# Three rotating places for queries and keys, and loads placed by the attention planner, in a fused attention, mixture and feed-forward kernel

## The chip, the cores and the metric

One core of a Trainium2 chip runs the whole program in one launch. The metric is the device time of one execution in microseconds (us); lower is better. The kernel before takes 396.39 us, the median of three runs (395.87 to 397.82).

## The reference

Three parts follow one another: windowed attention with a bias by distance, a soft mixture of experts whose dispatch is a softmax over all tokens, and a feed-forward layer with a squared ReLU. All data are float32.

```
# q, k, v: 4 batches, 8 heads, 576 positions, 64 wide
scores = q @ k.T / 8 - slope[h] * |i - j|     where 0 <= i - j < 128, else masked
attn   = softmax(scores) @ v                  -> x: 2304 tokens x 512
logits = x @ phi                              # 32 slots: 8 experts x 4
slots  = softmax(logits over tokens).T @ x
slots  = relu(slots[e] @ w1[e]) @ w2[e]       # 8 experts, 512 -> 1024 -> 512
x      = softmax(logits over slots) @ slots
out    = relu(x @ w_in) ** 2 @ w_out          # 512 -> 2048 -> 512
```

## The kernel before

Attention works in 16 **units** (a batch and a pair of heads) of 9 chunks of 64 queries. Two chunks make a **step**, 72 in all, so a unit has four and a half. For a step t, called S(t), T(t) and so on below:

- `emit_S` (L178, PE): the scores of two chunks, with up to 192 keys each; a chunk's Q is the weights (tile `zq`), K the moving side (`kt`). A float32 matmul shows as two passes in the trace, so a step has four.
- `emit_max` (L187, DVE) adds the bias and takes the row's extreme; `emit_exp` (L196, ACT) exponentiates and sums; `emit_sums` (L201, POOL) and `emit_recip` (L206, DVE) make the reciprocals, for two steps together except at either end; `emit_fold` (L220, POOL) and `emit_norm` (L228, POOL) fold and normalise p. Six buffers of p take turns.
- `emit_T` (L242, PE) transposes p, `emit_evac` (L262 on ACT, L266 and L268 on DVE) brings it to `ptb`.

When a unit's steps are through, `emit_PV` (L278, PE) multiplies by V into `xa` and `xb`, `emit_xT` and `emit_xTb` bring the result to `xT`, and `emit_X` (L321), `emit_Y`, `emit_logits` (L308), `emit_logr` (L314) and `emit_d0` to `emit_d4` keep the running mixture of each batch. After attention come 16 steps with the first expert matrices (L747, tile H), 16 with the second (L886, tile O) and the feed-forward (L939 and L983).

**The order** of attention is made by a planner. `op` records each operation with its engine, an assumed duration, what it comes after, a due time, the PSUM banks that it takes and a lag. `arrange` plays them on four engines' clocks, and takes each time the one that can start first, by due time among equals. `run` issues them in that order.

**The loads** all go through SP's queue, in the order in which they are written, but for three that ACT issues at the start. SP waits at a load until its place is free, and what stands behind it waits too. Per unit they are Z (the queries, 576 KB), K (288 KB) and V (320 KB). Z has two places, `zq[0]` and `zq[1]`, K two of its own, V two. Unit 2 alone uses a third for Z and K, the ring tile `first`. Weights go through a ring of 19 tiles of 1024 KB. During attention the ring is filled with 19 weight tiles, as 38 halves of 512 KB (`load_half_w`); five more go to space that attention leaves (`load_extra`), and one to `yw`.

Loads are not known to the planner. `run` adds them behind other operations: after the S that has a unit's last chunk, Z and K of the next unit for that place and two or three halves; after `emit_xTb` of u, V of u+2. The arrivals of the first units stand as times in `landed`.

## Time and profile before

| | us |
|---|---|
| median of three runs | 396.39 |
| lowest and highest | 395.87, 397.82 |
| the profiled execution, its own time | 395.99 |
| its span, first to last instruction | 394.0 |
| TensorE (PE) busy | 383.5, 97% of the span |
| VectorE (DVE), ScalarE (ACT), GpSimd (POOL) busy | 273.8, 245.7, 118.0 |
| the granted TensorE clock, mean of the span | 1.000 of full speed |

A profile tells of one execution. A row of the order of time has a start, a length, the engine, a line of the kernel and what that line writes and reads, and in brackets the idle time ahead of it with what ended it. Matmuls are pipelined and their ends are modelled, so that the lengths of neighbours overlap: the distance of starts tells how fast they go. A row of the waits has the total, the number of times and the longest. Engine names ending in q are queues that issue transfers.

### The profile page before, as it was taken

To read this page: it belongs to the slowest core of one execution; us is meant where nothing else is said; L and a number is where in the kernel's file an instruction comes from. 1 tells how busy PE (TensorE), PEld (TensorE's weight loads), DVE (VectorE), ACT (ScalarE), POOL (GpSimd) and SP (SyncE) were. 2 spreads that over 40 slices of the span, in tenths; PEclk is the share of its full clock that TensorE was granted. 3 is DMA by queue.
4 is the path that set the end of the run, shared out by engine and by line. 5 is a ranking of instruction groups with operands and counts; after the bars stand their busy time and mean duration, and the time that the engine had idled before them with its cause. 6 is when DMAs were issued, how large, how long until landed. Compare 5 with 4: busy or idle time off the path is not lost.

```text
span 394.0 us, 7876 instructions
## 1 busy us (share of the span) xinstructions
PE 383.5 (97%) x2602; PEld 299.9 (76%) x2602; DVE 273.8 (69%) x814; ACT 245.7 (62%) x730; POOL 118.0 (30%) x291
## 2 busy tenths in 40 slices
PE   8899999998998999999999999999999999999996
PEld 7788788787785435687787887888877888888884
DVE  5676776685774786387867788887867785566455
ACT  4989888887985212287776766777567544433440
POOL 4878667667663052122111212101010000000000
PEclk9999999999999999999999999999999999999999
DMA  7989999899899999999303200000000040003004
GB/s 233 373 291 357 330 322 408 284 326 409 269 358 353 418 426 426 417 416 406 119 0 108 108 0 2 0 0 2 0 0 3 0 161 2 0 31 130 0 1 161
DMA packets 23225, 75.36 MB, mean 191 GB/s; under 512 B 2832, under 2 KB 4624, under 8 KB 21520
## 3 DMA queue, kind: packets, MB, share of 16 engines
q1 hardware_dynamic: 22608, 74.30, 50.1%
q10 hardware_dynamic: 576, 0.56, 0.4%
q8 instruction: 21, 0.34, 0.3%
q14 instruction: 20, 0.16, 0.1%
HBM read 70.13 MB, written 4.72 MB: 190 GB/s over the span
## 4 chain that ended last, share of the span: by engine, by line
PE 88%; DMA 7%; DVE 2%; POOL 1%; ACT 1%; issue 1%; SPq 0%; DVEq 0%; POOLq 0%; ACTq 0%
PE acc L983 49%; PE s L178 10%; PE xa L278 6%; PE h L939 4%; DMA kt<-in_k_dram 4%; PE tp L242 4%; PE O L886 4%; DMA yw<-in_w_dram 3%; PE H L747 2%; PE X L321 2%; PE MX L835 1%; DVE psum L1001 1%; PE L L308 1%; PE xb L278 1%; PE R L374 1%
## 5 line engine op out<-in xcount | busy, mean ns | idle before, releaser
L983 PE MATMUL acc<-whl,arena_gh 128*128 128x512 f32 x864 | 216.5, 393 | 0.0
L983 PEld LDWEIGHTS acc<-whl,arena_gh 128*128 128x128 f32 x864 | 160.1, 188 | 35.3 <-issue 2.9
L968 DVE TENSOR_TENSOR arena_gh<-hT,arena_gh 128x384 fp32r<-128x384 f32 (+1 forms) x97 | 53.7, 553 | 30.1 <-ACT arena_gh L964 24.2
L196 ACT ACTIVATE p<-p,st 128x192 f32<-128x192 f32 (+1 forms) x144 | 61.6, 432 | 8.6 <-DVE st L187 6.2
L951 ACT ACTIVATE acc<-h 128x384 f32<-128x384 f32 x47 | 23.2, 493 | 64.9 <-PE h L939 64.9
L795 POOL TENSOR_SCALAR yw<-f 128x512 f32<-128x512 f32 x32 | 27.3, 857 | 100.4 <-DVE arena_cin L812 53.5
L228 POOL TENSOR_SCALAR p<-p,st 128x128 f32<-128x128 f32 (+1 forms) x142 | 49.9, 371 | 16.2 <-DVE st L206 10.7
L178 PE MATMUL s<-kt,zq 128*128 128x192 f32 (+2 forms) x270 | 50.7, 325 | 2.6 <-DMA kt<-in_k_dram 2.6
L187 DVE CUSTOM_DVE_ANT_0 p<-s,tbl 128x192 f32<-128x192 f32 (+1 forms) x144 | 42.1, 324 | 10.2 <-PE s L178 6.1
L178 PEld LDWEIGHTS s<-kt,zq 128*128 128x128 f32 x270 | 41.4, 197 | 4.0 <-DMA zq<-in_z_dram 2.9
L939 PE MATMUL h<-cst_sb,Mst 128*128 128x384 f32 x95 | 32.2, 339 | 0.1
L262 ACT ACTIVATE ptb<-tp 128x256 f32<-128x256 f32 (+1 forms) x72 | 25.0, 357 | 8.6 <-PE tp L242 8.4
L266 DVE TENSOR_SCALAR ptb<-tp 128x256 f32<-128x256 f32 (+1 forms) x64 | 24.4, 385 | 8.2 <-ACT ptb L262 8.0
L242 PE MATMUL tp<-cs,p 128*128 128x128 f32 x144 | 26.7, 282 | 2.2 <-POOL p L228 2.0
L220 POOL TENSOR_TENSOR p<-p 128x128 f32<-128x128 f32 (+1 forms) x64 | 27.1, 424 | 4.2 <-ACT p L196 1.3
L278 PE MATMUL xa<-ptb,vt 128*64 128x256 f32 (+1 forms) x256 | 27.8, 359 | 0.0
L196 ACT ACTIVATION_READ_ACCUMULATOR p<-p,st 128x1 f32 x144 | 27.7, 193 | 0.0
L960 DVE TENSOR_TENSOR hT<-acc 128x384 f32<-128x384 f32 x17 | 9.5, 557 | 23.2 <-ACT acc L951 23.2
L964 ACT ACTIVATE arena_gh<-hT 128x384 fp32r<-128x384 f32 x48 | 24.8, 517 | 0.7
L278 PEld LDWEIGHTS xa<-ptb,vt 128*64 128x64 f32 x256 | 17.0, 136 | 10.2 <-issue 2.9
L964 ACT ACTIVATE arena_gh<-acc 128x384 fp32r<-128x384 f32 x47 | 24.2, 516 | 0.6
L810 DVE SCALAR_TENSOR_TENSOR yw<-f,yw 128x512 int32<-128x512 int32 x32 | 22.4, 706 | 0.8
(205 smaller groups left out, 454.2 us busy)
## 6 DMA issues: line engine op xcount, KB each, us to landing
w_w<-in_w_dram SPq DMA_DIRECT2D x38, 512.0 KB, 7.4
w_w<-in_w_dram SPq DMA_DIRECT2D x12, 1024.0 KB, 9.3
f<-in_w_in_dram SPq DMA_DIRECT2D x16, 512.0 KB, 9.9
f<-in_w_out_dram SPq DMA_DIRECT2D x16, 512.0 KB, 10.0
zq<-in_z_dram SPq DMA_DIRECT2D x13, 576.0 KB, 5.2
vt<-in_v_dram SPq DMA_DIRECT2D x16, 320.0 KB, 6.6
kt<-in_k_dram SPq DMA_DIRECT2D x13, 288.0 KB, 5.6
out_dram<-psum SPq DMA_DIRECT2D x11, 256.0 KB, 2.0
```

The source lines that it names most:

```text
L178: pe.matmul(out=sb_t[t][:, 256 * i:256 * i + n], lhsT=zbuf(u)[:, c].rearrange("p a b -> p (a b)"), rhs=kt_t[u][:, 64 * c + 64 - n:64 * c + ...
L187: dve.tensor_tensor_reduce(out=p, in0=sb_t[t][:, 256 * i:256 * i + n], in1=tbl[:, 192 * pr + 192 - n:192 * pr + 192], scale=-0.125, scalar ...
L196: act.activation(out=p, in_=p, func=AF.Exp, bias=st[:, k + i:k + i + 1], scale=-1.0, accum_out=st[:, 4 + k + i:5 + k + i])
L220: pool.tensor_tensor(out=ap(True), in0=ap(True), in1=ap(False), op=ALU.subtract)
L228: eng.tensor_scalar(out=p, in0=p, scalar1=st[:, k + i:k + i + 1], scalar2=0.0, op0=ALU.mult, op1=ALU.add)
L242: pe.transpose(A[:, i, :], P[:, o:o + 128], ident)
L278: pe.matmul(out=out, lhsT=v_t[u][:, j, po:po + 64], rhs=pt[:, a:b, po:po + 64], start=(j == 0 or (j == 3 and a == 2)), stop=(j == 4 or (j ...
L795: pool.tensor_scalar(out=y.bitcast(F32), in0=t[:, a, :, 1].bitcast(F32), scalar1=2.0 ** -112, scalar2=0.0, op0=ALU.mult, op1=ALU.add)
L939: pe.matmul(out=hb[-1][:, 0:HB], lhsT=Mst[:, 128 * f:128 * f + 128], rhs=cst_sb[:, c0:c0 + HB], start=True, stop=True)
L964: act.activation(out=lo_t[i][1][hf][:, 0, cl], in_=rbuf[hf][:, cl], func=AF.Square)
L968: eng.tensor_tensor(out=gh[hf][:, 1, cl], in0=g[hf][:, cl], in1=gh[hf][:, 0, cl].bitcast(F32), op=ALU.subtract)
L983: pe.matmul(out=acc_t[s], lhsT=gh[:, x, c0:c0 + 128], rhs=w[:, f % 2, y, :], start=(units[i] in firsts and a == 0), stop=(units[i] in last ...
```

## The change

Z and K get three places each, taken in turn by u modulo 3 (`zslot`); the third is the tile `first`. The last of the 19 weight tiles takes that tile's place in the ring, so it can go only when unit 14's scores are done.

Loads of Z, K, V and phi, and the 38 halves, become operations of the planner on a fifth clock, SP, that starts at 8.2 us. Z and K come after the scores of all earlier units of their place, V after P times V of u-2, a half tile at an assumed time of 15 us and 2.4 us more for each. S then comes after its Z and K, `emit_PV` after its V. Assumed durations of the sums and of P times V, the transposes' lag, and the due times of S, the reciprocals, X and its copy are changed.

```diff
--- before.py
+++ after.py
@@ -128,7 +128,9 @@
     zpool = zt.enter_context(tc.tile_pool(name="zpool", bufs=1, side="right"))
     more, sx = ExitStack(), ExitStack()
     NQ = 2
+    NZ = 1
     zq = [zpool.tile([128, NCH, 2, 64], F32, name=f"zq{i}") for i in range(NQ)]
+    kq = [zpool.tile([128, S], F32, name=f"kq{i}") for i in range(NQ)]
     tbl = ppool.tile([128, 768], BF16, name="tbl")
     NP = 6
     pbuf = [ppool.tile([128, 384], F32, name=f"p{i}") for i in range(NP)]
@@ -142,17 +144,20 @@
 
     first = ring.tile([128, 3 * S], F32, tag="w", name="first")
 
+    zq.append(first[:, 0:2 * S].rearrange("p (c a b) -> p c a b", c=NCH, a=2))
+    kq.append(first[:, 2 * S:3 * S])
+
+    def zslot(u):
+        return u % (NQ + NZ)
+
     def zbuf(u):
-        return first[:, 0:2 * S].rearrange("p (c a b) -> p c a b", c=NCH, a=2) if u == 2 else zq[(u if u < 2 else u - 3) % NQ]
+        return zq[zslot(u)]
 
     def load_z(u, c0=0, c1=NCH, eng=sp):
         eng.dma_start(out=zbuf(u)[:, c0:c1].rearrange("p c a b -> p (c a b)"), in_=z[u, :, 128 * c0:128 * c1])
 
     def load_k(u, c0=0, c1=NCH, eng=sp):
-        if u == 2:
-            kt_t[u] = first[:, 2 * S:3 * S]
-        elif c0 == 0:
-            kt_t[u] = zpool.tile([128, S], F32, tag="kt", name="kt", bufs=NQ)
+        kt_t[u] = kq[zslot(u)]
         eng.dma_start(out=kt_t[u][:, 64 * c0:64 * c1], in_=k[u, :, 64 * c0:64 * c1])
 
     def load_v(u):
@@ -417,6 +422,9 @@
     pool.memset(lgT, -1.0e30)
     ops, users = {}, {}
 
+    def load_phi(a):
+        sp.dma_start(out=phi_sb, in_=phi)
+
     def op(f, arg, eng, ns, after=(), due=0, banks=(), lag=100, at=0):
         ops[f, arg] = {"at": at, "eng": eng, "ns": ns, "after": [x for x in after if x], "due": due, "banks": banks, "lag": lag}
 
@@ -431,18 +439,29 @@
             owner[u, j], last[slot] = last.get(slot), u
     fin = {u: (NCH * u + NCH - 1) // 2 for u in range(NU)}
     alone = (0, 1, NS - 2, NS - 1)
-    landed = {0: 0, 1: 900, 2: 2600, 3: 3500, 4: 5000, 6: 6000, 9: 10500, 13: 13500}
+    landed = {0: 0, 1: 900, 2: 2600, 3: 3500, 4: 5000, 6: 6000, 9: 10500}
+    steps_of = lambda u: range(NCH * u // 2, fin[u] + 1)
+    for u in range(1, NU):
+        if u > 2:
+            before = [x for y in range(u) if zslot(y) == zslot(u) for x in each(emit_S, *steps_of(y))]
+            op(load_z, u, "SP", 1450, before, STEP * fin[u - 1] - 20000, (), 2300)
+            op(load_k, u, "SP", 740, before, STEP * fin[u - 1] - 19990, (), 2300)
+        op(load_v, u, "SP", 810, each(emit_PV, u - 2)[:u > 1], STEP * fin[u] - 6000, (), 2300)
+    op(load_phi, 0, "SP", 200, (), 9000, (), 2300)
+    for j in range(2 * RING):
+        late = [u for u in range(NU) if zslot(u) == NQ + j // 2 - (RING - NZ)]
+        op(load_half_w, j, "SP", 1260, [x for u in late for x in each(emit_S, *steps_of(u))], 16000 + 2400 * j, at=15000 + 2400 * j)
     for t in range(NS):
         ch, t0 = info[2 * t:2 * t + 2], STEP * t
         two = [(t, 0), (t, 1)]
         steps = (t,) if t in alone else (t - 1, t) if t % 2 else (t, t + 1)
-        op(emit_S, t, "PE", sum(4 * n / 2.4 + 12 for u, c, n, e in ch), (), t0 - 1500, (("S", each(emit_max, *two)),), 200, max(x for y, x in landed.items() if y <= t))
+        op(emit_S, t, "PE", sum(4 * n / 2.4 + 12 for u, c, n, e in ch), [(f, u) for f in (load_z, load_k) for u, c, n, e in ch if u > 2], t0 - 3000, (("S", each(emit_max, *two)),), 200, max(x for y, x in landed.items() if y <= t))
         for i, (u, c, n, e) in enumerate(ch):
             op(emit_max, (t, i), "DVE", n / 0.96 + 72, each(emit_S, t) + each(emit_T, *range(t - NP, t - NP + 1)[:t >= NP]), t0 + 100 * i, (), 108)
             op(emit_exp, (t, i), "ACT", n / 1.4 + 303, each(emit_max, (t, i)), t0 + 400 + 100 * i, (), 170)
         if t == steps[0]:
-            op(emit_sums, (t, len(steps)), "POOL", 274, each(emit_exp, *[(x, i) for x in steps for i in range(2)]), STEP * steps[-1] + 1500, (), 0)
-            op(emit_recip, (t, len(steps)), "DVE", 90, each(emit_sums, (t, len(steps))), STEP * steps[-1] + 1600, (), 120)
+            op(emit_sums, (t, len(steps)), "POOL", 350, each(emit_exp, *[(x, i) for x in steps for i in range(2)]), STEP * steps[-1] + 1500, (), 0)
+            op(emit_recip, (t, len(steps)), "DVE", 90, each(emit_sums, (t, len(steps))), STEP * steps[-1] + 600, (), 120)
         whole = sum(x[2] == 192 for x in ch)
         if whole:
             op(emit_fold, t, "POOL", 164 + 138 * whole, each(emit_exp, *two), t0 + 1500)
@@ -452,7 +471,7 @@
         full = [(u, (c - 1) // 2) for u, c, n, e in ch if c]
         half = [(u, c // 2 if c % 2 == 0 else c // 2 - 1) for u, c, n, e in ch if c != 1]
         free = lambda l: each(emit_PV, *[owner[x] for x in l if owner[x] is not None])
-        op(emit_T, t, "PE", 222, each(emit_norm, *two), t0 + 3500, (("T", each(emit_evac, *two[:1 + bool(half)])),), 200)
+        op(emit_T, t, "PE", 222, each(emit_norm, *two), t0 + 3500, (("T", each(emit_evac, *two[:1 + bool(half)])),), 230)
         op(emit_evac, (t, 0), "ACT", 52 + 106 * len(full), each(emit_T, t) + free(full), t0 + 4000, (), 135)
         if half:
             op(emit_evac, (t, 1), "DVE", (0, 208, 342)[sum(x[1] > 1 for x in ch)] + 208 * sum(x[1] == 0 for x in ch), each(emit_T, t) + each(emit_evac, (t, 0)) + free(half), t0 + 4300, (), 120)
@@ -461,7 +480,7 @@
         t0, odd, late = STEP * fin[u], b % 2, u == NU - 1
         parts = [(t, i) for t in range(NCH * u // 2, fin[u] + 1) for i in range(2) if (emit_evac, (t, i)) in ops]
         old = (each(emit_X, u - 4) + each(emit_logr, (u - 4) // NPAIR)) if 4 <= u < NU - 4 + 2 else []
-        op(emit_PV, u, "PE", 1840, each(emit_evac, *parts), t0 + 5500, (("xa", each(emit_xT, u)), ("T" if late else "B", each(emit_xTb, u))), 190, 9500)
+        op(emit_PV, u, "PE", 1910, each(emit_evac, *parts) + each(load_v, u)[:u > 0], t0 + 5500, (("xa", each(emit_xT, u)), ("T" if late else "B", each(emit_xTb, u))), 190, 9500)
         op(emit_xT, u, "ACT", 477, each(emit_PV, u) + old, t0 + 7400, (), 165)
         op(emit_xTb, u, "DVE" if late else "ACT", 104, each(emit_PV, u) + old, t0 + 7450, (), 165)
         if late:
@@ -469,8 +488,8 @@
         x_all = each(emit_xT, u) + each(emit_xTb, u)
         if u < NU - 2:
             tag = "T" if kk == NPAIR - 1 else "B"
-            op(emit_X, u, "PE", 436, x_all, t0 + 9000, ((tag, each(emit_xn, u)),), 170)
-            op(emit_xn, u, "DVE", 608, each(emit_X, u) + each(emit_d3, b - 1)[:b], t0 + 9500)
+            op(emit_X, u, "PE", 436, x_all, t0 + 8000, ((tag, each(emit_xn, u)),), 170)
+            op(emit_xn, u, "DVE", 608, each(emit_X, u) + each(emit_d3, b - 1)[:b], t0 + 12500)
             if odd:
                 op(emit_Y, u, "PE", 109, each(emit_X, u), t0 + 9010, (("T", each(emit_xr, u)),), 170)
                 op(emit_xr, u, "ACT", 175, each(emit_Y, u) + each(emit_d3, b - 1)[:b], t0 + 9500)
@@ -496,7 +515,7 @@
             for x in o["after"]:
                 users.setdefault(x, []).append(k)
         ready, seen, order = {k: o["at"] for k, o in ops.items()}, {}, []
-        clock = dict.fromkeys(("PE", "DVE", "ACT", "POOL"), 0)
+        clock = {"PE": 0, "DVE": 0, "ACT": 0, "POOL": 0, "SP": 8200}
         held = {tag: [] for tag in NBUF}
         can = {e: [k for k in ops if ops[k]["eng"] == e and not wait[k]] for e in clock}
 
@@ -541,26 +560,15 @@
         if f in (emit_logits, emit_logr):
             for u in units_of(a):
                 f(u)
+        elif f is load_half_w:
+            f()
         else:
             f(*(a if isinstance(a, tuple) else (a,)))
         if f is emit_S:
             if a in (1, 3):
                 keep_warm("B", 1, idle)
-            for u, c, n, e in info[2 * a:2 * a + 2]:
-                if c == NCH - 1:
-                    nu = u + (3 if u < 2 else 2)
-                    if u != 2 and nu < NU:
-                        load_z(nu)
-                        load_k(nu)
-                    if u == 0:
-                        load_v(1)
-                        sp.dma_start(out=phi_sb, in_=phi)
-                    for _ in range(0 if u == 0 else 3 if u % 2 == 0 or u == 15 else 2):
-                        load_half_w()
         if f is emit_T and a == 0:
             keep_warm("B", 2, idle)
-        if f is emit_xTb and a + NQ < NU:
-            load_v(a + NQ)
 
     left = {f: sum(k[0] is f for k in ops) for f in (emit_S, emit_T, emit_norm)}
     for f, a in arrange():
```

What this moves shows in the programs' orders. **SP's queue, from unit 6's V (before) and from behind unit 8's K (after) on.** `vt` is V, `zq` Z, `kt` or `kq` K, `w_w` weights; a w's two rows are its two halves.

Before:

```order
L160 DMA vt_790<-in_v_dram 128x640
L149 DMA zq1_93<-in_z_dram 128x1152
L156 DMA kt_836<-in_k_dram 128x576
L88 DMA w_w19_838<-in_w1_dram 128x1024
L82 DMA w_w19_838<-in_w1_dram 128x1024
L88 DMA w_w111_841<-in_w1_dram 128x1024
L160 DMA vt_889<-in_v_dram 128x640
L149 DMA zq0_92<-in_z_dram 128x1152
L156 DMA kt_933<-in_k_dram 128x576
L82 DMA w_w111_841<-in_w1_dram 128x1024
L88 DMA w_w113_936<-in_w1_dram 128x1024
```

After:

```order
L82 DMA w_w15_688<-in_w1_dram 128x1024
L165 DMA vt_772<-in_v_dram 128x640
L88 DMA w_w17_787<-in_w1_dram 128x1024
L82 DMA w_w17_787<-in_w1_dram 128x1024
L88 DMA w_w19_837<-in_w1_dram 128x1024
L157 DMA zq0_92<-in_z_dram 128x1152
L161 DMA kq0_94<-in_k_dram 128x576
L165 DMA vt_893<-in_v_dram 128x640
L82 DMA w_w19_837<-in_w1_dram 128x1024
L88 DMA w_w111_929<-in_w1_dram 128x1024
L157 DMA zq1_93<-in_z_dram 128x1152
```

Before, V of unit 6 stands first, then Z and K of unit 8, three halves, V of unit 7, and Z and K of unit 9 in the place of unit 7. After, that V is the second row; Z and K of unit 8 stand ahead of these rows, and those of unit 9 in the place of unit 6, ahead of unit 7's V.

**PE, from T53 to T56.** The names p count the six buffers (the changed program's numbers are two higher), so T54 reads the first, T53 the last.

Before:

```order
L242 MATMUL tp<-cs,p_100 128x128 x2
L178 MATMUL s<-kt,zq_93 128x192
L178 MATMUL s<-kt,zq_92 128x64
L178 MATMUL s<-kt,zq_92 128x128
L178 MATMUL s<-kt,zq_92 128x192 x3
L278 MATMUL xa<-ptb,vt 64x256 x6
L278 MATMUL xa<-ptb,vt 64x128 x2
L278 MATMUL xb<-ptb,vt 64x64 x4
L242 MATMUL tp<-cs,p_95 128x128 x2
L242 MATMUL tp<-cs,p_96 128x128 x2
L242 MATMUL tp<-cs,p_97 128x128 x2
```

After:

```order
L247 MATMUL tp<-cs,p_102 128x128 x2
L183 MATMUL s<-kq_94,zq_92 128x192
L183 MATMUL s<-kq_95,zq_93 128x64
L247 MATMUL tp<-cs,p_97 128x128 x2
L183 MATMUL s<-kq_95,zq_93 128x128
L183 MATMUL s<-kq_95,zq_93 128x192
L247 MATMUL tp<-cs,p_98 128x128 x2
L183 MATMUL s<-kq_95,zq_93 128x192 x2
L283 MATMUL xa<-ptb,vt 64x256 x6
L283 MATMUL xa<-ptb,vt 64x128 x2
L283 MATMUL xb<-ptb,vt 64x64 x4
L247 MATMUL tp<-cs,p_99 128x128 x2
```

Before, S58, S59 and S60 stand together, then P times V of unit 11 (`xa`, `xb`), then T54, T55 and T56. After, T54 stands between S58 and S59, T55 between S59 and S60, and T56 alone behind P times V.

**PE at the end of attention, after P times V of unit 14.**

Before:

```order
L242 MATMUL tp<-cs,p_99 128x128 x2
L308 MATMUL L<-xT_102,phi_sb 32x128 x4
L308 MATMUL L<-xT_103,phi_sb 32x128 x4
L308 MATMUL L<-xT_104,phi_sb 32x128 x4
L242 MATMUL tp<-cs,p_100 128x128 x2
L314 MATMUL L<-xT_102,phi_sb 32x64
L314 MATMUL L<-xT_103,phi_sb 32x64
L314 MATMUL L<-xT_104,phi_sb 32x64
L278 MATMUL xa<-ptb,vt 64x256 x6
```

After:

```order
L247 MATMUL tp<-cs,p_100 128x128 x2
L247 MATMUL tp<-cs,p_101 128x128 x2
L247 MATMUL tp<-cs,p_102 128x128 x2
L313 MATMUL L<-xT_104,phi_sb 32x128 x4
L313 MATMUL L<-xT_105,phi_sb 32x128 x4
L313 MATMUL L<-xT_106,phi_sb 32x128 x4
L319 MATMUL L<-xT_104,phi_sb 32x64
L319 MATMUL L<-xT_105,phi_sb 32x64
L319 MATMUL L<-xT_106,phi_sb 32x64
```

T71 (the sixth p) stood between the two kinds of logits (`L`) of units 12 to 14; now T69, T70 and T71 come first and both kinds of logits after them. T68 now stands ahead of P times V of unit 14.

**POOL at the end of attention, from the fold of step 68 on.**

Before:

```order
L220 TENSOR_TENSOR p_97<-p_97 128x64
L201 TENSOR_SCALAR st<-st 128x4
L220 TENSOR_TENSOR p_98<-p_98 128x2x64
L201 TENSOR_SCALAR st<-st 128x2
L228 TENSOR_SCALAR p_97<-p_97,st 128x128 x2
L228 TENSOR_SCALAR p_98<-p_98,st 128x128 x2
L220 TENSOR_TENSOR p_99<-p_99 128x2x64
L228 TENSOR_SCALAR p_99<-p_99,st 128x128
L201 TENSOR_SCALAR st<-st 128x2
L220 TENSOR_TENSOR p_100<-p_100 128x2x64
L228 TENSOR_SCALAR p_100<-p_100,st 128x128
```

After:

```order
L225 TENSOR_TENSOR p_99<-p_99 128x64
L206 TENSOR_SCALAR st<-st 128x4
L225 TENSOR_TENSOR p_100<-p_100 128x2x64
L233 TENSOR_SCALAR p_99<-p_99,st 128x128 x2
L233 TENSOR_SCALAR p_100<-p_100,st 128x128 x2
L206 TENSOR_SCALAR st<-st 128x2
L225 TENSOR_TENSOR p_101<-p_101 128x2x64
L233 TENSOR_SCALAR p_101<-p_101,st 128x128
L206 TENSOR_SCALAR st<-st 128x2
L225 TENSOR_TENSOR p_102<-p_102 128x2x64
L233 TENSOR_SCALAR p_102<-p_102,st 128x128
```

The sums of step 70 (`st` of 128x2) stood ahead of the norms of steps 68 and 69; now they stand behind them.

## Rows read from the trace of the kernel before

**Rows 1.** The chain of work that ended last, its shares by engine (the page).
```profile
PE 88%; DMA 7%; DVE 2%; POOL 1%; ACT 1%; issue 1%; SPq 0%; DVEq 0%; POOLq 0%; ACTq 0%
```

**Rows 2.** Busy us of each engine by stage; then clock, DMA share, GB/s.
```profile
15.00:118.10 103.10, 100.53 (x968) 82.91 (x968) 72.97 (x389) 88.84 (x372) 73.94 (x219) 1.00 0.94 337
...
131.70:165.00 33.30, 33.13 (x419) 16.12 (x420) 21.77 (x62) 6.33 (x14) 8.88 (x10) 1.00 1.01 422
165.00:394.00 229.00, 225.24 (x1032) 181.84 (x1030) 162.86 (x290) 135.07 (x290) 23.13 (x27) 1.00 0.19 76
```

**Rows 3.** Waits of PE over the span: us in total, times, longest.
```profile
PE s L178 <- DMA kt<-in_k_dram: 2.6, 3, 1.6
PE tp L242 <- POOL p L228: 2.0, 2, 1.3
```

**Rows 4.** Order of time on PE (start, us, what) around units 9 and 13.
```profile
62.10 0.49 PE L178 MATMUL s<-kt,zq 128*128 128x192 f32 x2
63.34 1.01 PE L178 MATMUL s<-kt,zq 128*128 128x64 f32 x6 [0.75 <-DMA kt<-in_k_dram]
...
66.67 0.82 PE L178 MATMUL s<-kt,zq 128*128 128x192 f32 x4
67.32 0.38 PE L242 MATMUL tp<-cs,p 128*128 128x128 f32 x2
...
91.86 0.49 PE L178 MATMUL s<-kt,zq 128*128 128x192 f32 x2
93.99 1.66 PE L178 MATMUL s<-kt,zq 128*128 128x64 f32 x10 [1.65 <-DMA kt<-in_k_dram]
```

**Rows 5.** The chain in order of time, at the same two places.
```profile
56.77 6.44 DMA kt<-in_k_dram
...
86.67 7.18 DMA kt<-in_k_dram
```

**Rows 6.** Order of time on SP's queue: one V and two Z loads.
```profile
45.80 0.33 SPq L160 DMA_DIRECT2D vt<-in_v_dram  x1
...
50.25 0.33 SPq L149 DMA_DIRECT2D zq<-in_z_dram  x1
...
80.21 0.33 SPq L149 DMA_DIRECT2D zq<-in_z_dram  x1
```

**Rows 7.** Order of time on PE and POOL around steps 48 and 49.
```profile
78.82 0.82 PE L178 MATMUL s<-kt,zq 128*128 128x192 f32 x4
...
85.01 0.60 PE L242 MATMUL tp<-cs,p 128*128 128x128 f32 x4
...
83.47 1.37 POOL L228 TENSOR_SCALAR p<-p,st 128x128 f32<-128x128 f32 x4
```

**Rows 8.** Order of time on PE and POOL at the end of attention.
```profile
120.47 0.86 PE L308 MATMUL L<-xT,phi_sb 128*32 128x128 f32 x24
121.44 0.44 PE L242 MATMUL tp<-cs,p 128*128 128x128 f32 x2
...
116.31 0.46 POOL L220 TENSOR_TENSOR p<-p 128x128 f32<-128x128 f32 x1
117.34 0.19 POOL L201 TENSOR_SCALAR st<-st 128x2 f32<-128x2 f32 x1 [0.58 <-ACT p L196]
117.63 1.43 POOL L228 TENSOR_SCALAR p<-p,st 128x128 f32<-128x128 f32 x4
```

**Rows 9.** Order of time on SP's queue and PE, from attention to experts.
```profile
112.80 0.33 SPq L160 DMA_DIRECT2D vt<-in_v_dram  x1
...
116.32 10.17 SPq L97 DMA_DIRECT2D w_w<-in_w_dram  x5
...
138.94 1.06 PE L747 MATMUL H<-yw,siT 128*32 128x512 f32 x8
```

**Rows 10.** Busy us by stretch, as in rows 2.
```profile
25.00:111.00 86.00, 83.60 (x809) 68.86 (x809) 62.02 (x327) 74.24 (x309) 60.81 (x180) 1.00 0.94 339
116.30:139.00 22.70, 21.01 (x215) 11.76 (x219) 14.60 (x66) 9.47 (x33) 5.09 (x14) 1.00 0.98 375
```

## The prediction

> **What bounds the kernel now.** I read the chain of waits first: it runs through TensorE for 88% of the span and through transfers for 7% [rows 1]. Then the stages. Attention (15 to 118.1 us) has TensorE busy 100.53 of 103.10 us, with no other arithmetic engine above 89; the expert layers 33.13 of 33.30; the last feed-forward 225.24 of 229.00 [rows 2]. So TensorE sets the time in every stage, and a change of order gains only what TensorE idles today, or loses idle time that it makes.
>
> The waits of TensorE name that idle time: scores waited for a K transfer 2.6 us in three waits, transposes for POOL's normalised p 2.0 us in two [rows 3]. The order of time shows where: scores stop at 62.10 us after two passes of unit 8's last chunk and go on with unit 9 at 63.34; the same from 91.86 to 93.99, unit 12 to unit 13 [rows 4]. The chain goes through K's transfers there, 6.44 us from 56.77 and 7.18 us from 86.67 [rows 5]. They were issued only then because with two places in turn Z and K of unit u wait until unit u-2 has been read.
>
> **The change, part by part.** *K's waits.* A step's four score passes take 0.65 us from start to start (66.67 to 67.32), 0.16 each [rows 4]. From 62.10 to 63.34 are 1.24 us for two passes, so 0.91 idle; from 91.86 to 93.99 are 2.13, so 1.80. The gaps that the rows print (0.75 and 1.65) are smaller because a matmul's end is modelled; they give the low end, 2.40. With three places unit 9's Z waits for unit 6 and unit 13's for unit 10. Z loads that wait for just these units were issued at 50.25 and 80.21 [rows 6], 12 us before the scores at 62.1 and 91.9, where the longer K needed 7.18 [rows 5]. In the new queue one V and four half tiles stand between unit 8's K and unit 9's Z; that V went at 45.80 [rows 6], so all of them can go before 50.25. The third wait (0.2 us) belongs to the first load and stays. Both others go: **-2.7**, between -2.4 and -2.7.
>
> *The order of TensorE.* Scores and transposes are the same instructions; they now alternate where two or three stood together. A transpose of step t needs POOL's norm of t. In the sum of instruction times the tightest new place is T54: from S54 to T54 lie 2.63 of scores, 0.88 of four transposes, 1.9 of P times V and 0.5 of X, 5.9 us. Before, T48 came 6.19 us after S48, and its two norms (the first half of four in 1.37 us from 83.47) were done 5.4 us after S48 [rows 7]. So the tightest transpose still has some 0.5 us, and the long leads are cut without making the short ones shorter. In the first steps T5 moves ahead of S9, to right behind the place where T4 waits for POOL: nothing at best, at worst a second wait like the one of 1.3 us there [rows 3]. For all new waits of transposes I take **+0.2**, between 0 and 1.3.
>
> *The tail.* POOL's norms of steps 68 and 69 no longer stand behind the sums of step 70, which wait 0.58 us for an exponential: they could start at 116.77, when the fold before them ends (116.31 and 0.46), instead of 117.63; 0.86 earlier, of which the same sums, now behind the norms, take back 0.2 [rows 8]. T71 at 121.44 hangs on that chain: -0.7. But the logits of units 12 to 14, 24 passes that the row at 120.47 gives 0.86 us, filled the wait for T71 and now stand behind it, ahead of the last P times V [rows 8]: +0.8 with the modelled end off. I take **+0.1**; it is -0.7 if the logits hide after all, and +0.9 if T71 comes no earlier.
>
> *The first expert layers.* The step that reads yw begins at 138.94 [rows 9], 7.2 us into a stage in which TensorE idles 0.17 us in all [rows 2]; that bounds the wait for yw. It goes if yw lands earlier by more than attention ends earlier: **-0.1**, or 0. After the last score SP now has one extra tile, both halves of the nineteenth ring tile (its place is freed by unit 14), four extra tiles and yw: seven tiles of 1024 KB, 7.34 MB. From 113.6 us (116.32, when the first extra tile went, less 2.7 [rows 9]) to 136.2, when yw is wanted, at the 375 GB/s of that stretch [rows 10] 8.5 MB can come; 1.1 MB (2.9 us) to spare, if nothing else is left in the queue. Ahead of it, V of unit 15 and one half tile, 0.85 MB, wait for P times V of unit 13; that V went at 112.80 [rows 9], so at 110.1 now, and is through by 113.6.
>
> *Loads of V, phi, weights.* V keeps its two places and its wait for P times V of u-2; phi, 64 KB, now goes behind V of unit 1, and only the logits behind unit 3 need it; half tiles are wanted after 131 us. Each costs an issue on SP, which does no arithmetic: 0. No instruction of DVE, ACT or POOL is added; they had 72.97, 88.84 and 73.94 of 103.10 us to do [rows 2], and do the same in 2.5 us less.
>
> Sum: -2.7 + 0.2 + 0.1 - 0.1 = -2.5, against the profiled execution's 395.99 us (its span is 394.0): 393.5. The median of the runs is 0.4 above that execution, which would give 393.9; I say **393.6**. All low ends together (-3.5) give 392.5, all high ones (-0.2) 395.8.
>
> **The rivals.** *Transfers become the bound (20%).* From 25 to 111 us the new queue has to bring ten Z and K (864 KB each), thirteen V and 34 halves (512 KB each: of 38, two go before 25 us, where five did, and two after unit 14): 30.9 MB, 360 GB/s. The old one moved 339 in that stretch, at 0.94 of the engines' time [rows 10]. For it: 339/0.94 is 361, so no more than what is asked. Against: the expert stage moved 422 [rows 2], and a queue that is asked ahead of time is deeper. At 339 it is 1.75 MB behind at 111 us; that is 4.7 us at 375, of which 2.9 are spare, and the expert layers wait 1.8: 395.3; without the spare, 396 and more. The three places still hide Z and K, so this rival gives the gain back late and not in attention.
>
> *A ceiling of the queue (3%).* If 361 GB/s is what such a mixture can reach, in the last stretch too, and the queue idles as before, 1.75 MB take 4.8 us and the 7.34 MB 20.3 of the 22.6 us there; the expert layers wait 2.5: 396.0. Against it stand the 422 GB/s over 33 us [rows 2]. The Trainium skill (DMA: Bandwidth & Descriptors, section Where 436 GB/s comes from) has such a rule, some 358 GB/s for one core's loads from HBM, which speaks against a plan that asks for 360; by the 422 the trace does not agree with it.
>
> *K's or V's wait returns at other units (10%).* The change would then not do what it says: SP issues in order, and a Z ready to go can stand behind a V that waits for P times V. Against: unit 6's V, ahead of unit 9's Z, was free to go 4.4 us before it [rows 6]. About 396, no change.
>
> *Transposes wait for POOL (12%): slower.* The place is the run of single transposes from T46 to T56, and T12 and T20, with leads of 6.0 to 6.3 us. If norms end later than that after the scores, each waits, and everything behind it. For it: the first norm of a pair needs the exponentials of the step behind it too, and ACT is busy 86% of the stage [rows 2]. Against: such waits were 2.0 us in all, at the start and in the tail [rows 3]. Six of them at 1.3 us, the longest there is, make 7.8: 393.5 + 7.8 = 401.3; four of them, 398.7. It decides from 5.8 us between a score and its norm on; T48 shows 5.4.
>
> **How the numbers follow.** Forecast 52% (392.5 to 395, of that nine tenths below 394.4), transfers 20%, returning waits 10%, transposes 12%, the ceiling 3%, something I did not see 3%. A measurement of this kernel tells 0.5%, 2 us, from no change. Faster by more than that: 0.47 of the forecast and 0.03 of the transfers' rival, 0.50. Slower: the transposes and 0.02 of the unseen, 0.14. The same: the rest, 0.36. The range leaves out the worst transposes and what is unseen: 392.0 to 397.0; it takes in both signs, and the likeliest case's own is 392.5 to 395.
>
> **What would show it.** Right: no wait of scores for K but the first; unit 9's first score follows unit 8's last within 0.2 us; the step that reads yw starts near 136.3 with no wait; the last stage is as long as before (229 us). Transfers: the expert layers wait for yw or an extra tile. Transposes: PE waits for POOL's p in dozens, not two. The forecast is wrong if attention's end (the first expert step) does not come 2 to 3.5 us earlier than 131.7, or if it does and the span does not follow.

## Result, and the profile after

The kernel after the change takes **392.11 us** (median; 391.52 to 393.32), the kernel before on the same chip 396.96 us (395.87 to 398.57): a ratio of 0.9877, interval 0.985 to 0.9905. Two later comparisons, on other chips, gave 393.06 against 396.22 (0.9893, 0.9853 to 0.9933) and 393.08 against 396.5 (0.9913, 0.9891 to 0.9935). So the change is faster by 3.2 to 4.9 us; 393.6 was predicted. The profiled execution's span is 389.7 us, where before's was 394.0.

TensorE's share of the chain of waits is now 92%, the transfers' 1%, where [rows 1] had 88 and 7. The page's line:

```profile
PE 92%; ACT 2%; DVE 2%; POOL 2%; DMA 1%; issue 1%; DVEq 0%; POOLq 0%; ACTq 0%
```

The stages, columns as in [rows 2] (busy us and instructions of each engine, then granted clock, DMA share, GB/s): attention, expert layers, last feed-forward, and the stretch of [rows 10].

```profile
15.00:112.00 97.00, 96.98 (x939) 81.05 (x939) 70.41 (x379) 85.48 (x361) 72.12 (x213) 1.00 0.95 356
127.80:160.70 32.90, 32.89 (x419) 16.24 (x420) 21.77 (x61) 6.33 (x14) 8.80 (x10) 1.00 1.02 421
160.70:389.70 229.00, 225.27 (x1032) 181.86 (x1031) 162.87 (x290) 135.14 (x290) 23.11 (x27) 1.00 0.19 74
25.00:111.00 86.00, 86.00 (x841) 71.66 (x840) 62.55 (x334) 75.77 (x319) 63.79 (x188) 1.00 0.97 366
```

In the last row TensorE is busy all of the 86.00 us, where it was 83.60 [rows 10], and the queue moves 366 GB/s for 339. The last feed-forward takes the same 229.00 us.

The waits of TensorE over the span (us in total, times, longest). Two of K are left, both in the first 7 us; those at units 9 and 13 [rows 4] are gone:

```profile
PE tp L247 <- POOL p L233: 2.0, 3, 1.0
PE warm L112 <- DVE acc L396: 1.1, 1, 1.1
PE s L183 <- DMA kq<-in_k_dram: 0.7, 2, 0.5
PE X L644 <- ACT dT L639: 0.5, 1, 0.5
```

In order of time, where units 8 and 9 meet and where steps now alternate with transposes (units 12 and 13):

```profile
60.91 0.49 PE L183 MATMUL s<-first 128*128 128x192 f32 x2
61.24 0.33 PE L183 MATMUL s<-kq,zq 128*128 128x64 f32 x2
...
90.42 0.66 PE L183 MATMUL s<-kq,zq 128*128 128x192 f32 x4
90.92 0.39 PE L247 MATMUL tp<-cs,p 128*128 128x128 f32 x2
91.14 0.71 PE L183 MATMUL s<-kq,zq 128*128 128x128 f32 x4
```

Unit 9's scores follow two passes of unit 8 by 0.33 us, 0.16 a pass, where [rows 4] have 1.24 us and a wait. The end of attention on TensorE, which answers to [rows 8]:

```profile
113.05 0.68 PE L247 MATMUL tp<-cs,p 128*128 128x128 f32 x2 [0.42 <-POOL p L233]
...
116.85 0.44 PE L247 MATMUL tp<-cs,p 128*128 128x128 f32 x2 [0.64 <-POOL p L233]
117.22 0.86 PE L313 MATMUL L<-xT,phi_sb 128*32 128x128 f32 x24
```

The last transpose comes first now, and the 24 passes of logits behind it, as the instruction order said.

One table carries what follows. All times are starts of TensorE's instructions in the order of time, in us: where step 4's first score starts; from there to the first expert step; from that to the step that reads yw; from the second expert layer's first step to the last matmul.

| execution | step 4 | to first expert step | to yw's step | rest |
|---|---|---|---|---|
| before | 9.86 | 121.86 | 7.22 | 242.02 |
| before, once more (f4) | 9.69 | 123.05 | 7.93 | 242.37 |
| after | 9.21 | 118.60 | 6.86 | 242.01 |
| after, once more | 9.57 | 118.55 | 7.78 | 241.99 |
| after, third (f3) | 9.51 | 118.55 | 8.16 | 242.04 |
| e1: three places alone | 9.60 | 119.18 | 6.86 | 242.03 |
| e3: all but the due times | 9.61 | 119.18 | 7.71 | 241.98 |
| e4: due times alone | 9.59 | 120.35 | 6.86 | 242.03 |
| f1: three places and due times | 10.37 | 118.55 | 7.44 | 241.99 |
| e2: the change with two places | 9.11 | 121.80 | 6.86 | 242.01 |
| f2: the change, halves earlier | 9.70 | 118.57 | 6.87 | 241.99 |
| f2 once more (g2) | 9.21 | 118.55 | 6.86 | 242.02 |
| g1: the change, halves later | 9.61 | 118.55 | 11.59 | 242.05 |

The second column repeats within 0.05 us among executions that give TensorE the same order and don't wait for a transfer. The first and the third vary from execution to execution; why, and what of it is the change's doing, is what the experiments had to say.

### The profile page after: what moved, and what is told of

It reads as the page before. It is cut to its first block, busy times and chain, and to the rows that moved or that the text cites. A ratio compares the mean times of both kernels' runs of the same rounds, so it can differ in the third digit from the quotient of the medians.

```text
span 389.7 us, 7880 instructions
## 1 busy us (share of the span) xinstructions
PE 381.3 (98%) x2602; PEld 299.3 (77%) x2602; DVE 273.7 (70%) x814; ACT 244.7 (63%) x730; POOL 117.9 (30%) x291
## 4 chain that ended last, share of the span: by engine, by line
PE 92%; ACT 2%; DVE 2%; POOL 2%; DMA 1%; issue 1%; DVEq 0%; POOLq 0%; ACTq 0%
PE acc L991 50%; PE s L183 10%; PE xa L283 6%; PE h L947 4%; PE tp L247 4%; PE H L755 4%; PE O L894 4%; PE X L326 2%; ACT p L201 1%; PE L L313 1%; PE MX L843 1%; DVE psum L1009 1%; PE xb L283 1%; POOL p L233 1%; PE R L379 1%; DMA kq<-in_k_dram 1%
## 5 line engine op out<-in xcount | busy, mean ns | idle before, releaser
L183 PE MATMUL s<-kq,zq 128*128 128x192 f32 (+2 forms) x198 | 38.1, 320 | 0.7 <-DMA kq<-in_k_dram 0.7
L183 PEld LDWEIGHTS s<-kq,zq 128*128 128x128 f32 x198 | 30.3, 194 | 1.7 <-DMA kq<-in_k_dram 1.2
L247 PE MATMUL tp<-cs,p 128*128 128x128 f32 x144 | 28.1, 281 | 2.2 <-POOL p L233 2.0
L247 PEld LDWEIGHTS tp<-cs,p 128*128 128x128 f32 x144 | 18.2, 143 | 7.0 <-POOL p L233 4.8
```

The lines of the kernel that those rows point to most:

```text
L183: pe.matmul(out=sb_t[t][:, 256 * i:256 * i + n], lhsT=zbuf(u)[:, c].rearrange("p a b -> p (a b)"), rhs=kt_t[u][:, 64 * c + 64 - n:64 * c + ...
L247: pe.transpose(A[:, i, :], P[:, o:o + 128], ident)
```

## Experiments

**First, the change in parts.** On one chip, before at 396.22 us.

*e1: three places, due times as before.* The queue is still written by hand; Z and K of unit u+3 are asked for where those of u+2 were. TensorE's instructions come in the order of before.

```diff
+    kq = [zpool.tile([128, S], F32, name=f"kq{i}") for i in range(NQ)]
...
+    zq.append(first[:, 0:2 * S].rearrange("p (c a b) -> p c a b", c=NCH, a=2))
+    kq.append(first[:, 2 * S:3 * S])
...
-        return first[:, 0:2 * S].rearrange("p (c a b) -> p c a b", c=NCH, a=2) if u == 2 else zq[(u if u < 2 else u - 3) % NQ]
+        return zq[u % 3]
...
-                    nu = u + (3 if u < 2 else 2)
-                    if u != 2 and nu < NU:
+                    nu = u + 3
+                    if nu < NU:
```

> The old order of every engine and the old hand-written order of the queue, with three places for Z and K in turn. Theory A (the third place alone takes K's two waits away): no wait of scores for K at units 9 and 13, the first expert step 2.7 us earlier than 131.7, ratio 0.993, about 2.7 us less. Rival C (it takes the planner's queue, because halves stand ahead of Z): at least one of the two waits stays, ratio 0.998 to 1.0. Rival B (the new order of work makes most of the 4.3 us by which the spans differ) says no more than 1.5 us here.

Measured: 393.21 us (392.42 to 394.75), ratio 0.9894 (0.9851 to 0.9937). From step 4 to the first expert step 119.18 us, 2.68 less than before. Its one wait for K:

```profile
PE s L179 <- DMA kq<-in_k_dram: 0.2, 1, 0.2
```

The third place alone takes both waits away, and that is most of the gain. (The profile is of e1's slowest run, 394.75 us. What is slower there lies behind the last matmul, outside the table: the last two stores land after 4.2 us, in before's profile after 1.9.)

*e3: the change with the due times and durations of before.* The arithmetic engines get the order of before, the planner orders the loads.

```diff
-            op(emit_sums, (t, len(steps)), "POOL", 350, each(emit_exp, *[(x, i) for x in steps for i in range(2)]), STEP * steps[-1] + 1500, (), 0)
+            op(emit_sums, (t, len(steps)), "POOL", 274, each(emit_exp, *[(x, i) for x in steps for i in range(2)]), STEP * steps[-1] + 1500, (), 0)
...
-            op(emit_X, u, "PE", 436, x_all, t0 + 8000, ((tag, each(emit_xn, u)),), 170)
+            op(emit_X, u, "PE", 436, x_all, t0 + 9000, ((tag, each(emit_xn, u)),), 170)
```

The due times of the scores, the reciprocals and xn, the lag of the transposes and the duration of P times V go back in the same way.

> The changed kernel with the old due times and assumed durations: the order of PE, DVE, ACT and POOL is the old one, three places, and the queue ordered by the planner. Theory A: as the third place alone, ratio 0.993 within 0.002, since Z and K come in time either way. Rival C: 0.993 here but not with the hand-written queue. If the planner's queue also brings yw and the extra tiles sooner, up to 0.3 us more than with the hand-written queue.

Measured: 393.55 us (392.84 to 394.41), ratio 0.9908 (0.9875 to 0.9941). Attention takes 119.18 us, as in e1: who orders the queue changes nothing there. But TensorE waits for yw:

```profile
PE H L755 <- DMA yw<-in_w_dram: 0.6, 1, 0.6
```

*e4: before with the change's due times and durations,* the reverse of e3's edit; two places, queue by hand.

> The kernel before with the new due times and durations alone: the order of PE, DVE, ACT and POOL is that of the changed kernel, the queue and the two places are the old ones. Theory A: K's waits stay (2.4 us or more in two), the tail is 0.2 to 0.7 us shorter, T4 and T5 at the start change little: ratio 0.996 to 0.999. Rival B: the start and the tail give 1.5 us or more, ratio 0.996 or less, and with the third place's share the parts add to the whole.

Measured: 394.78 us (393.13 to 397.15), ratio 0.9955 (0.9925 to 0.9986). Attention 120.35 us, 1.51 less than before. K's waits stay, but shrink to 0.75 us at unit 9 and 0.56 at unit 13, where 2.4 or more in two was expected:

```profile
PE s L178 <- DMA kt<-in_k_dram: 1.5, 3, 0.7
```

Why they shrink wasn't tried.

*The change once more.*

> The changed kernel once more, on the same chip as its parts. Ratio 0.988 within 0.003. Its profile and those of the three others tell whether the first 9 us are the change's: TensorE's passes of 192 columns go from 0.32 to 0.16 us apart near 5 us in the changed kernel's profile and near 7.5 us in that of before, with the same instructions ahead. Theory A: this moment varies from one execution to the next, whatever the kernel, and the 0.6 us of it are not the change's. Rival: it goes with the order of work (early in this kernel and in the one with new due times alone, late in the two with the old order).

Measured: 393.06 us. Attention 118.55 us, 0.63 less than e1's, so the new order itself gains; and here, too, TensorE waits for yw, 0.7 us, which it did not in the first execution. By the medians, 393.06 and 393.21, the change was no faster than e1 on this chip. The trace has TensorE's full clock from 7.8 us on, not from 4.9 as in the first execution, with the same order of work: so the expectation's rival, that this moment goes with the order, fell. Two questions were left: does the order gain, and why does yw vary?

**Second: order and yw.** On one chip, before at 396.5 us.

*f1: e1 and e4 together,* that is the change's order and places with the hand-written queue.

> The kernel before with three places and with the new due times, but with its hand-written order of loads: TensorE, VectorE, ScalarE and GpSimd get the instructions of the change in the order of the change; the transfers are queued as in e1. Theory 1 (the queue that the planner writes costs the change 0 to 0.9 us at yw, and the new order of TensorE gains about 0.6 us before the expert layers): first expert step at 127.8 to 128.3 us, the step that reads yw 6.86 us behind it with no wait, and a time 0.3 to 0.9 us below the change's and 0.5 to 0.9 us below e1's, so some 392.3 where the kernel before is at 396.2. Theory 2 (the new order gains nothing, and the 0.66 us between e1 and the change is chance): first expert step at 128.6 to 128.9 like e1, time as e1's. Theory 3 (only the planner's queue lets the new order gain): a wait for K or V comes back, first expert step after 128.6 us.

Measured: 391.89 us (391.53 to 393.18), ratio 0.989 (0.9868 to 0.9912). Attention 118.55 us, exactly the change's, and 0.63 under e1's, which differs from it in the due times alone: the gain of the order is no chance. The first expert step came at 128.92, outside what was expected, because step 4 started as late as 10.37 (below). And yw was not free of waiting: 7.44, with a wait of 0.4 us. So theory 1 held for the order, and not for its "no wait": the hand-written queue, too, is at the edge. Yet by the medians of six runs each, whose ranges overlap, f1 is 1.2 us faster than the change on the same chip (393.08, in f3 below), more than the 0.3 to 0.9 that theory 1 had: the planner's queue did not gain, it cost.

*f2: one condition more in the planner.* The change makes half tile j wait, in the plan, for the units whose place is numbered NQ + j // 2 - 18. Only the nineteenth tile (j // 2 = 18) takes a place that Z and K had, the third. By the formula the seventeenth and eighteenth wait for the first two places as well; the first is used by unit 15, so two halves wait in the plan for the last scores. Half tiles are issued in the order of the ring, whichever j the plan calls, and so it is the nineteenth tile's halves that end up behind the first extra tile.

```diff
-        late = [u for u in range(NU) if zslot(u) == NQ + j // 2 - (RING - NZ)]
+        late = [u for u in range(NU) if j // 2 >= RING - NZ and zslot(u) == NQ + j // 2 - (RING - NZ)]
```

> The change with one condition more in the planner: half weight tiles whose place was never Z's or K's do not wait in the plan for scores. All four arithmetic engines get the change's order; SP issues all 38 halves before the first extra tile, where the change issues two (1 MB) behind it. Theory 1 (yw is late because 1 MB that could have gone in the hole from 96 to 103 us stands in the 8 us ahead of the last extra tiles): the step that reads yw comes 6.86 us after the first expert step, no wait of TensorE for yw or an extra tile, and 0 to 0.9 us less than the change on the same chip. Theory 2 (yw is late by the speed of the transfers in that execution, whatever stands ahead): 6.9 to 7.8 us here too, the change's time. Theory 3 (half tiles issued earlier stand in front of Z, K or V): a wait for K of over 0.3 us, and a first expert step later than the change's by as much.

Beside it the change again:

> The change itself once more, beside f1 and f2 on one chip. Both theories: 392 to 393.1 where the kernel before is at 396.2, ratio 0.988 to 0.991; first expert step 127.7 to 128.2 us; the step that reads yw 6.9 to 7.8 us later. The rise of TensorE's granted clock lay at 4.9 and at 7.8 us in two executions of it; if it is chance, it lies anywhere between here.

Measured: f2 391.88 us (six runs from 391.48 to 391.96), ratio 0.9886 (0.9867 to 0.9905); the change on that chip 393.08 (391.95 to 393.49). Attention is the same, 118.57 and 118.55; the whole of it is yw. SP's queue of the change in f3, in order of time, with the last half tiles (L88, L82) behind the first extra tile (L97), and the step of TensorE that reads yw:

```profile
112.72 0.33 SPq L97 DMA_DIRECT2D w_w<-in_w_dram  x1
113.10 0.43 SPq L88 DMA_DIRECT2D w_w<-in_w_dram  x1
113.57 0.43 SPq L82 DMA_DIRECT2D w_w<-in_w_dram  x1
...
117.69 0.33 SPq L97 DMA_DIRECT2D w_w<-in_w_dram  x1
...
136.22 1.06 PE L755 MATMUL H<-yw,siT 128*32 128x512 f32 x8 [1.09 <-DMA yw<-in_w_dram]
```

The same in f2:

```profile
110.19 0.42 SPq L82 DMA_DIRECT2D w_w<-in_w_dram  x1
112.93 0.33 SPq L97 DMA_DIRECT2D w_w<-in_w_dram  x1
117.92 0.33 SPq L97 DMA_DIRECT2D w_w<-in_w_dram  x1
...
135.13 1.07 PE L755 MATMUL H<-yw,siT 128*32 128x512 f32 x8
```

What the transfers do from 112 to 136 us, in 40 slices of 0.6 us (busy share in tenths, then GB/s). f3, the change:

```profile
DMA  8897798699999999997999999999999999989999
GB/s 137 273 314 239 253 355 328 280 355 300 328 376 410 389 403 416 403 341 287 423 410 382 423 437 410 437 423 437 437 423 423 437 423 437 389 355 416 430 403 423
```

And f2:

```profile
DMA  9939299940094999959999999999999998999999
GB/s 379 396 137 218 55 423 423 437 191 0 0 150 96 382 410 437 410 137 396 437 437 423 423 437 437 437 423 437 423 423 410 410 437 369 335 389 382 437 423 423
```

In f2 the queue runs empty near 117.5 us, before the last extra tiles and yw are asked for (from 120.6 on in f3, yw at 123.1 in f2); in f3 it never does. yw takes 13.3 us from issue to landing in f3, 10.0 in f2. The two halves of f2 went out at 96.47 and 97.49, ahead of a V that waits for P times V; SP stands at that V until 103.4, and in f3 from 96.2 to 103.2. What the transfers moved meanwhile (columns as in [rows 2]), f3 and then f2:

```profile
98.00:103.00 5.00, 5.00 (x69) 4.22 (x58) 3.53 (x24) 4.61 (x23) 2.85 (x9) 1.00 0.72 257
98.00:103.00 5.00, 5.00 (x70) 4.23 (x62) 3.74 (x24) 4.61 (x22) 2.87 (x9) 1.00 1.03 409
```

So 1 MB moved into a time in which the transfers had room is what separates a wait of 1.1 us from none. In the same 5 us the hand-written queues of e1 and f1 move 405 and 403 GB/s, the planner's, in the change's three executions, e3 and g1, 250 to 279.

*f4: before once more, for its profile.*

> The kernel before once more, for its profile alone. Theory 1 (the moment at which TensorE is granted its full clock in the first 9 us is chance, and no doing of the change): it can lie anywhere from 4.9 to 7.9 us here as well; whatever it is, K's two waits are 2.4 to 2.7 us and the first expert step comes at 131.2 to 131.8 us, the earlier the earlier the clock. Theory 2 (the change's first steps set it): it lies at 7.9 again and the first expert step at 131.7.

Measured, in its one run: 398.08 us. Step 4 starts at 9.69. K's waits are larger than in the first profile, and a fourth stands at unit 5 (0.3 us):

```profile
PE s L178 <- DMA kt<-in_k_dram: 3.5, 4, 1.6
PE tp L242 <- POOL p L228: 2.3, 3, 1.3
...
PE H L747 <- DMA yw<-in_w_dram: 0.9, 1, 0.9
```

Attention took 123.05 us, 1.2 more than in the profile that the prediction used, and the first expert step came at 132.74, where 131.2 to 131.8 was expected; yw was late here as well. Before's waits for transfers vary between its two profiles; that this is why its runs lie between 394.7 and 400.3 us, while f2's lie within half a microsecond, is likely and not shown.

**Third: the cost doubled, a repeat, and the third place taken away.** On one chip, before at 396.35 us.

*g1: more halves behind.*

```diff
-        late = [u for u in range(NU) if zslot(u) == NQ + j // 2 - (RING - NZ)]
+        late = [u for u in range(NU) if zslot(u) == (0 if j >= 32 else -1)]
```

> The suspected cost doubled: in the change, four half tiles (2 MB) instead of two (1 MB) are issued behind the first extra tile, and two of them behind the second; the order on the arithmetic engines is the change's. Theory 1 (what the queue has still to bring when the last extra tiles are asked for decides when yw comes): 1 MB more at 0.42 MB a us is 2.5 us; the step that reads yw comes 9.3 to 10.7 us after the first expert step, where the change had 6.9 to 8.2, and the time is 1.5 to 2.5 us over the change's: 394.5 to 395.5. Theory 2 (yw's time is chance): 6.9 to 8.2 us and the change's time, 392 to 393.5. From step 4's first score to the first expert step 118.55 us under both.

Measured: 398.0 us (396.55 to 399.27), ratio 1.0043 (1.0019 to 1.0067): slower than before. yw's step comes at 11.59. Theory 1 is right in kind and too low in size: six halves instead of three now stand behind V of unit 15, 1.57 MB more, not 1; at the 0.42 MB a us of that stretch 3.7 us, and 11.59 is 3.4 behind f3's 8.16. The profiled execution's span, 395.3 us, is 4.0 over f3's; another 0.5 of it lies between yw's step and the second expert layer, which come 9.50 us apart instead of 9.04. TensorE's waits:

```profile
PE H L755 <- DMA w_w<-in_w_dram: 2.7, 2, 1.9
...
PE H L755 <- DMA yw<-in_w_dram: 0.6, 1, 0.6
```

and the four microseconds around them (columns as in [rows 2]):

```profile
137.00:141.00 4.00, 3.19 (x16) 0.59 (x20) 1.61 (x3) 0.69 (x1) 1.74 (x2) 0.57 1.01 417
```

TensorE, which had waited 1.85 us before 137.26, ran these 4 us at a granted clock of 0.57, mostly the lower of its two levels (1.2 GHz), and at 1.00 again from 141 us on. The median is 0.8 us over the profiled run (397.18); the slowest runs have a mean clock of 0.991, the profiled one 0.996.

*f2 once more.*

> f2 once more, on another day of the chip. Theory 1: no wait for yw in this profile either, 6.87 us from the first expert step to the one that reads yw, and 391.5 to 392 where the kernel before is at 396.5. Theory 2: a wait of 0.4 to 1.1 us for yw in this profile, and 392.5 to 393.5. From step 4's first score to the first expert step 118.55 us under both.

Measured: 391.84 us (391.56 to 391.89), ratio 0.9871 (0.9838 to 0.9904); no wait for yw, 6.86. f2 beats the change and the kernel before.

*e2: the change with two places.*

```diff
     def zslot(u):
-        return u % (NQ + NZ)
+        return u if u <= 2 else (u - 3) % NQ
```

> The change with its third place taken away again (Z and K of unit 2 in the ring tile, all others in two places in turn); queue by the planner, new due times, orders on the arithmetic engines within some 20 rows of the change's. Theory 1 (K's waits hang on the number of places alone): TensorE waits for K at units 9 and 13 as in e4, 1.3 to 2 us in all; from step 4's first score to the first expert step 119.9 to 120.6 us, where the change has 118.6, and a time 1.2 to 2 us over the change's. Theory 2 (the planner, which now sees the loads, issues them early enough with two places too): no wait for K but the first, 118.6 to 119 us, the change's time.

Measured: 395.59 us (394.61 to 398.34), ratio 0.9986 (0.9955 to 1.0017). Attention 121.80 us, 3.2 over the change; the waits for K:

```profile
PE s L183 <- DMA kq<-in_k_dram: 2.5, 5, 0.9
```

Theory 1 is right in kind, and the size was missed again: one of the five waits is the first load's (0.4 us), the others lie at units 5, 8, 9 and 13. TensorE's order differs from the change's in 73 of 2602 places, so not all of the 3.2 us need be the places'. With two places the planner's queue is worse than the hand-written one (e4: 120.35): without the third place the change would have gained nothing that can be measured.

## Why the prediction was right, and where not

The direction, the main cause and its size were right; the number is 1.5 us too high against the first comparison and 0.5 against the other two. That the first, 392.11, lies inside the range is owed to luck: it is 0.1 us from its end, and under the 392.5 to which all low ends add. By the prediction's own sign the forecast missed, too: the first expert step was to come 2 to 3.5 us earlier than 131.7 and came at 127.81, 128.12 and 128.06, 3.6 to 3.9 earlier. By its steps:

- **K's waits, -2.7: right.** e1 shows -2.68 with the order of TensorE unchanged. The reading of [rows 4], 0.91 and 1.80 from start to start instead of the printed 0.75 and 1.65, gave the size that came. One thing it could not see in one execution: the price itself varies, as f4's 3.5 us in waits shows, and it hangs on the order: with the change's due times two places cost 1.80 (e4 against f1, 120.35 and 118.55).
- **Order of TensorE, +0.2 (0 to 1.3): wrong sign.** With K's waits gone, the due times take 0.63 us (f1 against e1, 118.55 and 119.18). The step that failed is the bound of 0: the reasoning looked only for waits that the new order could make, and not for idle time that the old one had. The 0.63 lie in three places. *Steps 4 to 9:* T4 stands 4.9 us behind step 4's first score instead of 5.5, the likely cause being POOL's fold of step 6, which by the instruction order now stands behind the norms of steps 4 and 5. But T5, now right behind T4, waits for its own norm: S9 starts 6.05 us behind step 4 instead of 5.92, and T5's two passes take some 0.2 of that. So T5 ahead of S9, "nothing at best" in the prediction, gave 0.1. *S9 to S71:* 96.32 for 97.03 us; some 0.4 of this is four passes that moved out, T5's and, to behind S71, T67's; the other 0.3 is idle time in small pieces, between scores and transposes that stood in groups. *S71 to the first expert step:* 16.18 for 16.22 us with T67's two passes in it, so another 0.3 of idle. Which neighbours give the pieces wasn't tried.
- **Tail, +0.1: right,** and for its reasons. From S71 to the first expert step before took 16.25, after 16.21. T71 comes 0.72 earlier behind S71 (5.25 for 5.97; -0.7 was said), and the logits take back 0.68 (+0.8). That T67 comes behind S71 was not seen; what it takes is counted above.
- **First expert layers, -0.1 (0 to -0.17): wrong in both bounds.** Without any wait yw's step comes 6.86 us in, 0.36 sooner than the 7.22 of before: the 0.17 us that the row of that stage leaves idle [rows 2] did not bound the wait, since the passes ahead of it are drawn as busy to their modelled ends. Before's weight load of that step does show a wait for yw (1.1 us, row below). And it can come later: 7.78 and 8.16 in two of the change's three executions. The 2.9 us of spare were not there. They were counted as if the queue could be asked for all 7.34 MB from 113.6 us on; but the extra tiles go out one by one as attention's memory comes free (112.45, 117.44, from 120.35 on), and by f2, f3 and g1 what is still in the queue at that time decides. That is the rival of transfers, with a wait of 0 to 1.1 us where 1.8 was said, and by another way: not by the rate in attention, which rose to 366 GB/s, but by 1 MB that went behind V of unit 15 and not into the room ahead of it. f2 and g1 show it from both sides.
- **V, phi, loads of weights, 0: right in attention** (e3 equals e1 to 0.01 us), and for the half tiles wrong at yw, as just told: their place cost 1.2 us by the medians (393.08 in f3, 391.88 in f2).
- **The first 9 us: not in the prediction.** Step 4 starts at 9.21 in the change's first profile and 9.86 in before's. With the change's due times it came at 9.11 to 10.37 in nine executions, with those of before at 9.60 to 9.86 in four: nothing shows that any of the 0.65 us is the change's.

The rows behind two of these readings: T4, in the change once more (step 4 at 9.57) and in e1 (9.60),

```profile
14.47 1.31 PE L247 MATMUL tp<-cs,p 128*128 128x128 f32 x4 [0.99 <-POOL p L233]
...
15.06 0.62 PE L243 MATMUL tp<-cs,p 128*128 128x128 f32 x2 [1.33 <-POOL p L229]
```

and before's wait for yw, on the weight loads of TensorE (PEld):

```profile
PEld H L747 <- DMA yw<-in_w_dram: 1.1, 1, 1.1
```

The two profiles add up: -0.65 at the start, -3.26 in attention, -0.36 in the expert layers, 0 behind them, -4.27 of 4.3. Of it the change's own, by e1, f1 and the repeats: -2.7 for the places, -0.6 for the order, and -0.4 to +0.9 at yw.

The other rivals: *waits of transposes for POOL* did not come (2.0 us in three waits, where before had 2.0 in two). *K's wait at other units* did not come. *A ceiling of the queue* at 361 GB/s is refuted by 366 over 86 us and 421 over the expert stage. The Trainium skill (DMA: Bandwidth & Descriptors, section Where 436 GB/s comes from) puts some 358 GB/s as the limit of one core's loads from HBM; these rows do not agree with it.

## What to carry to other kernels

A wait that shows in one place of the trace, for a load whose buffer came free too late, was worth here what it lasts from start to start, and a third buffer took it away whole, under both queues (e1, e3). When loads are put into a planner, compare with the queue that was there: here the places and the order gained, and the planner's queue cost about 1.2 us (f1 against f3) until f2 mended it. Look at the last things it issues before a change of stage: 1 MB cost nothing where the transfers had room and a microsecond in front of the tile that was wanted next, and the plan's wait must be that of the tile which is really issued. A new order is weighed against the idle time that the old one has, not only against what it may add.

## What the hardware showed that was not expected

*TensorE's rise to its full rate* comes at another moment in each execution of the same program. The trace's records of the granted clock begin, at 1.00, at 4.89, 7.82 and 7.15 us in the change's three executions, and at 9.26 in f1's, which gives TensorE the same instructions; ahead of that they have nothing (the clock column of a stretch prints 1.00 there too). The four passes of step 2's scores in the change's first execution, in order of time, and under them those of steps 2 and 3 in f1's:

```profile
6.35 0.92 PE L183 MATMUL s<-kq,zq 128*128 128x192 f32 x4 [0.49 <-DMA kq<-in_k_dram]
```

And f1:

```profile
6.59 1.49 PE L179 MATMUL s<-kq,zq 128*128 128x192 f32 x4
...
9.28 0.82 PE L179 MATMUL s<-kq,zq 128*128 128x192 f32 x4
```

Passes of 192 columns start 0.32 us apart before the rise (0.16 behind it): the lower and the higher of the two levels, 1.2 and 2.4 GHz. In the change the step at 6.35 already runs at the full rate; in f1 not before the step at 9.28. Step 4 came 1.2 us apart (9.21 and 10.37), about as much as the longest wait at yw; 0.14 of it was there at the first score (3.73 and 3.87). Differences of one or two profiles below a microsecond are therefore taken from a point behind the rise.

*A busy queue is not a full one.* Two stretches of f3, columns as in [rows 2]:

```profile
112.00:117.00 5.00, 4.06 (x37) 2.75 (x35) 3.40 (x17) 3.90 (x16) 4.22 (x13) 1.00 0.87 278
120.00:136.00 16.00, 14.40 (x139) 7.51 (x135) 11.86 (x50) 6.10 (x18) 0.79 (x1) 1.00 1.00 407
```

At a share of 0.87 the first moves 278 GB/s; the same share of the second's rate would be 354. A plan that counts bytes by the rate of the best stretch has less room than it thinks. Why the first is slower wasn't tried.
